# Frequency filter and SwiGLU block on one Trainium2 core: the inverse transform's last stage on 32x32 parts, in one burst a chunk

## Chip, cores and metric

One Trainium2 chip, one core. The metric is device time in microseconds of one launch, the median of three runs. The engines carry their usual names: TensorE (PE in the profile, its weight loads PEld), VectorE (DVE), ScalarE (ACT), GpSimd (POOL) and SyncE (SP), which issues most of the DMAs. Each engine works through its own instructions in order and waits on semaphores for the others.

## What is computed

The reference does two things, one after the other, all in float32:

```python
X = np.fft.rfft(x, axis=1)                       # x: (8, 3008, 256)
y = np.fft.irfft(X * (filt_r + 1j * filt_i)[None], n=3008, axis=1)
x = y.reshape(24064, 256)
g, val = x @ w_gate, x @ w_val                   # 256 -> 1536
out = (g * sigmoid(g) * val) @ w_out             # 1536 -> 256
```

The weights arrive as float64 and are rounded on the chip at the start. There are 8 batches of 3008 tokens.

## The kernel before

**Two pipelines in one order.** For each batch the filter is a Fourier transform written as matrix products. 3008 is 47 x 64, so there is a first stage over 47 points, a second over 64, the filter, and the same two backwards. While the block after it (the SwiGLU products) works on batch b, the transforms of batch b + 1 are slipped in between. A batch's tokens are cut into 4 chunks (`NCHUNK`), the hidden units into 3 groups (`NG`), so a batch takes 12 steps, and step s works on chunk s // 3 and group s % 3.

**The order is written by hand.** Every step goes once through the list `SCHEDULE`, token by token, and each token issues a few instructions on their engines; `pin` keeps them in that order. A quote at the end of a token (`S00'`) means the step before. These are the tokens that matter here:

- `P`, `Q`, `A`, `B`, `E` are products with the weights on TensorE (four records of 188 columns each). The pairs 01, 02, ... belong to a scheme that saves products at the price of sums.
- `f`, `c`, `m`, `g`, `u` are ScalarE's copies and SiLUs. `x`, `s`, `y`, `e`, `l` prepare or correct a PSUM bank on VectorE or ScalarE. So `s13` (or `x03`) must be done before product `A13` can add to its bank.
- `h` and `v` are VectorE's products of the two halves of a pair. They fill the two `h` tiles of the step. `h03` and `v03` are the last of a step.
- `S00` to `S31` are GpSimd's sums of `h` slots, `D` its differences, and `W1` to `W7` are the products with `w_out`, which read `h` and those sums a step later. `o` and `z` gather their results, `x0.o` to `x5.o` and `i` store them.
- `n1`, `n2`, `n3` call `combine_sequence`: sums of a new chunk's `y` into `y_t`, which A, B and E products read.
- `t0.0` to `t4.3` and `b0` to `b7` take one piece each of the next batch's transforms, from the lists `plan` and `bursts`. `quads` (first stage, steps 0 to 3) and `fours` (second stage and its inverse, steps 4 to 10) come through `b`; `first_fold` in step 11.

At the end of a step the order is `E03 n1 t4.1 v01 g23 B03 l03 W3 h23 g03 u03 h03 v03`, and the next one begins `Q0 o3' z1.o' t4.2' W2 b0 f0 S00' S01' i0 b1 b2`.

**The stage that changes.** `back(k, m)` is the inverse's last step, 47 points from 24 frequencies, for chunk k. Its input is tile `t4` (`load_t4`, two tiles a chunk, read from DRAM with two DMAs each: one for the tokens with h = 0 on partitions 0 to 47, one for h = 1 on partitions 64 to 111). On each half the 24 cosine rows and 24 sine rows lie one below the other, so one product of 48 rows yields 32 of the 47 points: m = 0 gives points 0 to 31, m = 1 points 15 to 46 (`LATER` = 15; the overlap is computed twice). Table `back_t` holds the two 48 x 32 tables for each half. One call issues 16 products (2 tiles x 4 channel parts x 2 halves; each fp32 product shows as two matmul records) into 2 PSUM banks. Two VectorE transposes of 32 x 32 blocks (L1049) bring these into `y`. After m = 1 GpSimd makes four sums in place in `y` (the lines at L312 and L315 for `y<-y`), which the products need.

The calls are placed by `plan`: for chunks 1, 2, 3 in steps 1, 4 and 7 of their batch, m = 0 at `t2.0` and m = 1 at `t3.1`; for chunk 0 in step 11 of the batch before, at `t0.0` and `t2.0`. `t4` is loaded at the head of steps 0, 2, 5 and at `B01` in the same steps; chunk 0's in step 10 at `A12` and `E23`. Batch 0 uses another routine (`stage3`) and isn't touched, but its step 11 holds batch 1's first chunk.

Of the kernel before, what the change touches and what calls it, by code (L numbers as in the profile page):

```python
# [41 lines left out]
FP32 = mybir.dt.float32  # L42
# [11 lines left out]
N1, N2 = 47, 64  # L54
# [31 lines left out]


SCHEDULE = """
Q0 o3' z1.o' t4.2' W2 b0 f0 S00' S01' i0 b1 b2 x0.o' t0.0 x1.o' i1 Q1 P0 t0.1 x2.o' P3 x3.o' f1 t4.3'
W1 x4.o' S10' x03 S11' D01 i2 i3 i4 s13 b3 x5.o' P1 o1 b4 t0.2 o2 z0.o c1 i5 A13 g1 c0 S20' Q2  # L90
S21' g0 y01 m13 t1.0 h0 f2 s01 W6 t1.1 h1 x23 D02 P2 o6 D12 A01 t0.3 i6 c2 i7 B13 i8 g2 i9 n3' m01
i10 S30' t1.2 i11 x02 W7 S31' g13 y12 y02 B01 h13 o7 t1.3 t2.0 s02 s12 g01 h2 b5 Q3 t2.1 h01 e12
A02 y23 W4 e02 b6 y03 m02 g3 A12 o4 z2.o t2.2 E12 m12 B02 t2.3 l12 e13 b7 E02 u12 g02 t3.0 h3 s23
l02 B12 v12 E13 t3.1 h02 u02 A23 n2 l13 g12 v02 W5 s03 e23 h12 e01 m23 A03 o5 z3.o u13 E23 t3.2 m03
v13 E01 l23 e03 t3.3 t4.0 l01 u23 B23 v23 u01 E03 n1 t4.1 v01 g23 B03 l03 W3 h23 g03 u03 h03 v03
""".split()
KS = (-1, 0, 1, 2)

# [11 lines left out]
SLOT = {p: i for i, p in enumerate(ORDER)}  # L110
SUM = {f"{z}{i}{j}": 6 * e + n for e, z in enumerate("ABE") for n, (i, j) in enumerate(PAIRS)}
NPR = len(ORDER)

LATER = N1 - 32

PIECES = ((0, 7), (7, 14), (14, 20), (20, 26))

# [4 lines left out]
def dft_tables():  # L122
# [27 lines left out]
    hi = 2 * np.pi * (np.outer(2 * n1 + 1, s) % (2 * N1)) / (2 * N1)  # L150
    scale = np.where(s == 0, 1.0, 2.0) / S
    one_hi = np.concatenate([np.cos(hi) * scale, -np.sin(hi) * scale * (s > 0)], 1).T
    back = np.zeros((128, 2, 32))
    for h, table in enumerate((one, one_hi)):
        for m in range(2):
            back[64 * h:64 * h + 2 * NS, m] = table[:, LATER * m:LATER * m + 32]
    back = back.reshape(128, 64)

    quad = np.zeros((4, 32, 2, 32))
    for h in range(2):  # L160
# [40 lines left out]
def kernel(  # L201
# [357 lines left out]
    def load_back():  # L559

        t = rpool.tile([128, 2, 128], U32, name="quad", tag="pw", bufs=3)
        t = t.bitcast(FP32).rearrange("p b f -> p (b f)")
        quad_t.append(t)
        pin(nc.sync.dma_start(out=t[:, 0:65], in_=quad_dram.ap()))
        t = rpool.tile([128, 2, 128, 2], U32, name="back", tag="raw", bufs=2)
        t = t.bitcast(FP32).rearrange("p b f two -> p (b f two)")
        back_t.append(t[:, 0:64])
        pin(nc.sync.dma_start(out=back_t[0], in_=back_dram.ap()))


# [10 lines left out]
    class Spectral:  # L581
# [82 lines left out]
        def load_t4(self, k, i, part=None):  # L664
            at = 2 * k + i
            if part:
                self.load_rows(self.t4[k, i][8 * N_STORED:NK], k, slice(2 * N_STORED, NS), ts(i, NH))
                return
            t = t4pool.tile([128, NH, C], FP32, name=f"t4_{self.b}_{k}_{i}", tag="t4")
            if part == 0:  # L670
                self.load_rows(t[0:8 * N_STORED], k, slice(0, 2 * N_STORED), ts(i, NH), nc.gpsimd)
            elif self.b == 0:
                self.load_rows(t[0:NK], k, slice(0, NS), ts(i, NH))
            else:

                rows = self.d2_tokens.rearrange("(h n) a c -> h a n c", h=2)
                for h in range(2):
                    self.load(out=t[64 * h:64 * h + 2 * NS], in_=rows[h, :, ts(at, NH)])
            self.t4[k, i] = t

        def bank(self, name):
# [346 lines left out]

        def back(self, k, m):

            if m == 0:
                self.y[k] = ypool.tile([128, 8, TQ], FP32, name=f"y_{self.b}_{k}", tag="y")
            y = self.y[k]
            banks = [bank(f"pd_{self.b}_{k}_{m}_{h}") for h in range(2)]
            outs_ = [t.rearrange("p (z i n d) -> p i z n d", z=2, i=2, d=32) for t in banks]
            for i in range(2):
                t = self.t4[k, i].rearrange("p n (z j d) -> p j z n d", z=2, d=32)
                for j in range(4):  # L1040
                    for h in range(2):
                        r = slice(64 * h, 64 * h + 2 * NS)
                        pin(nc.tensor.matmul(  # L1043
                            out=outs_[h][32 * j:32 * j + 32, i], lhsT=back_t[0][r, ts(m, 32)],
                            rhs=t[r, j], start=i == 0, stop=True, skip_group_check=True))
            yield
            to = y.rearrange("p s n -> p (s n)").rearrange("p (z h m r) -> p h z m r", z=2, h=2, r=N1)
            for h in range(2):
                pin(nc.vector.transpose(  # L1049
                    out=to[:, h, :, :, LATER * m:LATER * m + 32],  # L1050
                    in_=banks[h].rearrange("p (z m d) -> p z m d", z=2, d=32)))
                if h == 0:
                    yield
            for a in range(4 if m else 0):
                b, v = y[:, a], y[:, 4 + a]
                for _ in range(abs(KS[a])):
                    pin((sub if KS[a] > 0 else add)(nc.gpsimd, v, v, b))
# [33 lines left out]
    class Group:  # L1091
# [94 lines left out]
        def project(self, op, last=False):  # L1186
# [9 lines left out]
            if kind in "xXi":  # L1196
                t, cb, step = outs[b, k], int(kind == "X"), 2 if last else 1
                if kind == "x" and q < NG - 1 and takes_turns(b, k) and p == 5:
                    pin(nc.sync.dma_start(out=o_dram[k], in_=t))
                if q == NG - 1 and (b or kind == "i"):  # L1200
                    some = (p,) if kind == "i" else (2 * p, 2 * p + 1)
                    for n, (u, cq) in enumerate(divmod(m, 4) for m in some):
                        rows = min(32, NR - 32 * u)
                        at = (b * S + 32 * 32 * u + 2 * NH * k) * C + 128 * cb + 32 * cq
                        queue = nc.sync if b else nc.gpsimd
                        if last:
                            queue = (nc.sync, nc.scalar, nc.gpsimd)[(2 * p + n) % 3]
                        pin(queue.dma_start(  # L1208
                            out=bass.AP(tensor=out.tensor, offset=out.offset + at,
                                        ap=[[32 * C, rows], [128 * step, 4 * NH // step], [1, 32]]),  # L1210
                            in_=t[32 * cq:32 * cq + rows, cb::step, ts(u, 32)]))
                return
# [159 lines left out]


    older = before = None
    gap = iter(())
    pieces_before = []

    def order_of(b):
# [24 lines left out]
            yield  # L1403


    def later(piece):

        yield
        yield from piece

    def chain(*pieces):

# [30 lines left out]
    for b in range(B):  # L1443
# [2 lines left out]
        plan = [[] for _ in range(NCHUNK * NG)]  # L1446

        def three(s, k, cur=cur):
            if s.b == 0:
                return [s.stage3(k, step) for step in range(4)]  # L1450
            return [s.back(k, m) for m in range(2)]

        d = [three(cur, k) for k in range(1, NCHUNK)]
        one = [] if b else [nxt.stage1(u) for u in range(N_ONE)]
        bursts = [[] for _ in range(NCHUNK * NG)]
        if b and nxt:
            for n in range(N_QUAD // 2):
                bursts[n] = nxt.quads(n)
            for n in range(N_FOUR + 1):
                bursts[N_QUAD // 2 + n] = nxt.fours(n)  # L1460
        if b + 2 < B:
            bursts[-1] = following.first_fold()
        bursts = [iter(p) for p in bursts]
        two = []
# [2 lines left out]
            two += [nxt.stage2a(u)] if u < N_TWO else []  # L1467
        if nxt:
            gap = iter(())
            first = three(nxt, 0)  # L1470
            plan[11] = [first[0], gap, first[1]]
            if b:
                plan[1], plan[4], plan[7] = [[gap, gap, p[0], later(p[1])] for p in d]
            if b == 0:
                for k in range(NCHUNK - 1):
                    plan[k] = d[k] + one[k:k + 1]
                plan[0] = [gap, d[0][0], chain(d[0][1], d[0][2]), d[0][3], one[0]]
                plan[3], plan[4], plan[5] = one[3:8], one[8:13], one[13:16]
# [3 lines left out]
        else:  # L1482
            plan[1], plan[4], plan[7] = [[gap, gap, p[0], later(p[1])] for p in d]

        for step in range(NCHUNK * NG + (b == B - 1)):
            ghost = step == NCHUNK * NG
# [15 lines left out]
            for place, token in enumerate(SCHEDULE):  # L1502
                if b == 0 and this and place in tick_at[min(step, 3)]:
                    preparation.tick(step)
                old = token.endswith("'")
# [14 lines left out]
                elif op[0] == "t":  # L1520
                    n = int(op[1])
                    ps = pieces_before if old else pieces
                    if n < len(ps):
                        next(ps[n], None)
                elif op[0] == "b":
                    next(bursts[step] if this else gap, None)
                elif op[0] in "Wo" or op.endswith(".o"):
# [19 lines left out]
                if b and chunk and op == "B01":  # L1547
                    cur.load_t4(chunk, 1)
                for i in range(2):
                    if nxt and (step, op) == (10, ("A12", "E23")[i] if b else "E23"):  # L1550
                        nxt.load_t4(0, i)
                for f, args in chores.get((step, op), ()) if b == 0 else ():
                    f(*args)
                if op in ends and not last and (b or step >= NT * NG - 1):
                    reload_weights((g + 1) % NG, ends[op])
            older, before, pieces_before = before, this, pieces
    for op in LAST:
# [32 lines left out]
```

## Time and profile before

| | |
|---|---|
| median of three runs | 2787.48 us (2787.07 to 2790.02) |
| profiled execution | 2790.41 us |
| its span, first to last instruction | 2788.6 us |
| mean granted TensorE clock | 0.997 |
| records of `back` (L1043) | 1792 matmuls, mean 382 ns, busy 61.4 us |
| transposes of `back` (L1049) | 112, mean 707 ns |
| sums in `y` on GpSimd | 112 of 188 elements, 0.59 to 0.61 us each |
| loads of `t4` (`t<-d`) | 112 of 192 KB on SP's queue |

The profile is of one execution. Its first part gives busy time by engine. "Busy" counts a matmul from its start to its modelled end, and matmuls overlap, so TensorE's 99% is no measure of how fast it goes; the distance from one start to the next is. The chain is the work that ended last, followed back from the end: at each step to whatever released it. Groups (line, engine, operation, output<-inputs, shape, count) give busy time, mean duration of one, and the idle time before them. A timeline lists instructions by start, with equal neighbours merged; the brackets behind a row tell how long the engine had been idle and what ended that.

W2 stands near the head of every step (`wF<-h` in the profile), so the distance between two of its starts is the length of a step.

### The profile page before, as it was taken

How to read it: one execution, taken by the hardware profiler on the slowest of the kernel's cores; microseconds unless marked ns; L12 is line 12 of the kernel's file. 1: busy time of each engine (PE TensorE's matmuls, PEld its weight loads, DVE VectorE, ACT ScalarE, POOL GpSimd, SP SyncE). 2: the span in 40 equal slices, each digit the busy share in tenths (PEclk: the TensorE clock that was granted, in tenths of full speed). 3: DMA queues.
4: the chain of work that ended last, by engine and by line, in shares of the span. 5: the costliest groups of instructions: out<-in, count | busy, mean ns of one | idle time of the engine just before them, and what ended most of it. 6: DMA issues, size and time to landing. Idle time of an engine off the chain costs nothing.

```text
span 2788.6 us, 51410 instructions
## 1 busy us (share of the span) xinstructions
PE 2748.3 (99%) x16952; PEld 2249.3 (81%) x16952; DVE 2081.7 (75%) x4703; ACT 1514.6 (54%) x4086; POOL 1647.4 (59%) x1801
## 2 busy tenths in 40 slices
PE   8999999999999999999999999999999999999998
PEld 6777887888878888788878888878887888888886
DVE  7888777777687777777778777777777777676666
ACT  5776454555555555555555555555554555555553
POOL 4786576566545665556654566555655566555554
PEclk9999999999999999999999999999999999999999
DMA  8688877878676776777767777668767677655543
GB/s 216 218 273 267 282 240 243 265 243 263 205 211 208 253 244 190 212 238 229 247 184 233 220 249 223 207 194 264 243 213 201 215 239 237 183 156 147 156 137 83
DMA packets 383488, 608.47 MB, mean 218 GB/s; under 512 B 197118, under 2 KB 266652, under 8 KB 383048
## 3 DMA queue, kind: packets, MB, share of 16 engines
q1 hardware_dynamic: 364410, 574.18, 65.9%
q10 hardware_dynamic: 16174, 25.50, 3.6%
q0 software_dynamic: 2640, 5.51, 0.7%
q8 instruction: 137, 2.24, 0.3%
q14 instruction: 127, 1.04, 0.1%
HBM read 484.45 MB, written 118.12 MB: 216 GB/s over the span
## 4 chain that ended last, share of the span: by engine, by line
PE 89%; DVE 3%; POOL 2%; ACT 1%; DMA 1%; issue 1%; SPq 0%; POOLq 0%; DVEq 0%; ACTq 0%
PE wa L1125 25%; PE wk L1125 17%; PE wA L1223 16%; PE we L1125 12%; PE wG L1223 8%; PE wF L1223 4%; PE wpd L1043 2%; PE wqc L807 1%; PE wqb L819 1%; PE wqa L727 1%; POOL h L315 0%; POOL out_dram L1208 0%; PE wpa L889 0%; DVE we L315 0%; DVE y L319 0%
## 5 line engine op out<-in xcount | busy, mean ns | idle before, releaser
L1125 PE MATMUL wa<-y_t,wt_t 128*128 128x188 f32 x4464 | 883.5, 324 | 10.5 <-DVE wa L1147 5.5
L1125 PEld LDWEIGHTS wa<-y_t,wt_t 128*128 128x128 f32 x4464 | 746.0, 190 | 102.9 <-issue 14.7
L1125 PEld LDWEIGHTS wk<-y,wt_t 128*128 128x128 f32 x2976 | 494.4, 190 | 125.2 <-issue 36.7
L1125 PE MATMUL wk<-y,wt_t 128*128 128x188 f32 x2976 | 575.6, 326 | 1.4 <-ACT f L1140 1.4
L315 POOL TENSOR_TENSOR h<-h 128x376 f32<-128x376 f32 x572 | 560.1, 1000 | 15.1 <-DVE h L312 14.9
L1223 PE MATMUL wA<-h,wo_t 128*128 128x376 f32 x1532 | 549.0, 481 | 3.4 <-POOL h L315 1.8
L1125 PE MATMUL we<-y_t,wt_t 128*128 128x188 f32 x2232 | 432.4, 323 | 2.4 <-DVE we L319 1.6
L315 POOL TENSOR_TENSOR D<-f,f 128x376 f32<-128x376 f32 x288 | 280.5, 985 | 252.0 <-ACT f L1140 245.4
L312 POOL TENSOR_TENSOR h<-h 128x376 f32<-128x376 f32 x190 | 183.2, 984 | 408.0 <-DVE h L1172 402.2
L315 DVE TENSOR_TENSOR we<-we,m 128x376 f32<-128x376 f32 x576 | 317.3, 552 | 91.6 <-PE we L1125 51.4
L1125 PEld LDWEIGHTS we<-y_t,wt_t 128*128 128x128 f32 x2232 | 369.1, 190 | 4.9 <-DVE we L319 2.8
L1223 PEld LDWEIGHTS wA<-h,wo_t 128*128 128x128 f32 x1532 | 278.0, 190 | 106.6 <-POOL h L315 5.4
L1160 ACT COPY m<-wa 128x376 f32<-128x376 f32 x576 | 275.4, 478 | 110.8 <-PE wa L1125 105.0
L1167 ACT ACTIVATE u<-we 128x188 f32<-128x188 f32 x576 | 188.9, 328 | 188.5 <-DVE we L315 179.1
L1223 PE MATMUL wG<-h,wo_t 128*128 128x376 f32 x768 | 273.9, 479 | 0.0
L319 DVE SCALAR_TENSOR_TENSOR y<-wk,c 128x376 f32<-128x376 f32 x480 | 246.7, 540 | 33.7 <-ACT c L1144 29.5
L1167 ACT ACTIVATE g<-wa 128x188 f32<-128x188 f32 x576 | 187.4, 326 | 143.8 <-PE wa L1125 141.6
L1144 ACT COPY c<-wk 128x376 f32<-128x376 f32 x288 | 136.9, 475 | 234.5 <-PE wk L1125 228.1
L1156 ACT COPY we<-y 128x376 f32<-128x376 f32 x480 | 218.9, 480 | 42.9 <-DVE y L1049 24.7
L1140 ACT ACTIVATE f<-wk 128x376 f32<-128x376 f32 x288 | 145.1, 504 | 168.6 <-PE wk L1125 108.3
L1172 DVE TENSOR_TENSOR h<-we,u 128x188 f32<-128x188 f32 x576 | 198.7, 345 | 35.1 <-ACT u L1167 21.9
L1172 DVE TENSOR_TENSOR h<-wa,g 128x188 f32<-128x188 f32 x576 | 196.1, 344 | 26.2 <-ACT g L1167 26.1
(194 smaller groups left out, 3532.0 us busy)
## 6 DMA issues: line engine op xcount, KB each, us to landing
wt_t<-w_all SPq DMA_DIRECT2D x174, 896.0 KB
wt_t<-w_all SPq DMA_DIRECT2D x174, 768.0 KB
lent<-filter SPq DMA_DIRECT2D x36, 1024.0 KB
quads<-lent SPq DMA_DIRECT2D x96, 256.0 KB
d<-lent ACTq DMA_DIRECT2D x84, 256.0 KB
t<-d SPq DMA_DIRECT2D x112, 192.0 KB
lent<-quads SPq DMA_DIRECT2D x144, 128.0 KB
lent<-raw SPq DMA_DIRECT2D x144, 128.0 KB
```

The costliest lines, as they stand in the source:

```text
L312: return eng.tensor_tensor(out=dst, in0=a, in1=b, op=ALU.add)
L315: return eng.tensor_tensor(out=dst, in0=a, in1=b, op=ALU.subtract)
L319: return nc.vector.scalar_tensor_tensor(out=dst, in0=a, scalar=-1.0, in1=b, op0=ALU.mult, op1=ALU.subtract)
L1043: pin(nc.tensor.matmul(out=outs_[h][32 * j:32 * j + 32, i], lhsT=back_t[0][r, ts(m, 32)], rhs=t[r, j], start=i == 0, stop=True, skip_group ...
L1125: pin(nc.tensor.matmul(out=ps[:, z], lhsT=self.wt[:, SLOT[p], z], rhs=rhs, start=start and z == 0, stop=True, skip_group_check=True))
L1140: pin(act.mul(self.small(f"f{i}", f"f{i}", 1), t[f"k{i}"], -1.0))
L1144: pin(act.copy(out=self.small(f"c{i}", f"c{i}", 1), in_=t[f"k{i}"]))
L1156: pin(act.copy(out=self.bank(f"e{at}"), in_=t[f"y{at}"]))
L1160: pin(act.copy(out=self.small(f"m{at}", "m", 4), in_=t[f"a{at}"]))
L1167: pin(act.activation(out=self.small(op, "g", 3, 1)[:, 0], in_=ps[:, 1], func=AF.Silu))
L1172: pin(v.tensor_tensor(out=dst, in0=ps[:, 0], in1=g, op=ALU.mult))
L1223: pin(nc.tensor.matmul(out=self.tiles[at], lhsT=wo_t[:, JB * q + i, WO[p], :], rhs=self.hs[i][:, HID[p]], start=start and i == 0, stop=Tru ...
```

## The change

1. `back` takes a whole chunk in one call. Cosine and sine rows are parted: `t4` is loaded with four DMAs a tile, 24 rows each, to partitions 0, 32, 64 and 96 (h = 0 cosine, h = 0 sine, h = 1 cosine, h = 1 sine), and `back_t` holds four 24 x 24 tables. Each of four parts gives 24 points, and 32 products (2 x 4 x 4, 32 columns of output, 24 rows in, 256 columns long) go to four PSUM banks.
2. The cosine banks are transposed by VectorE straight into `y`. The sine banks are copied to SBUF by ScalarE and transposed there in place by VectorE. Then GpSimd makes points 24 to 46 as cosine minus sine, mirrored, and points 0 to 23 as cosine plus sine in place, four sums a chunk. The four old sums in `y` follow.
3. New tokens `r0` to `r5` place the pieces. `r0` (the burst) stands between `l03` and `W3` at the end of steps 0, 3, 6 (chunks 1, 2, 3) and 10 (chunk 0 of the next batch); `r1` (transposes and copies) before `h03`; `r2'` to `r5'` in the step that follows. The calls in `plan` go. Batch 1's chunk 0 goes through `bursts` in step 11 of batch 0, beside `first_fold`.
4. Chunk 0's `t4` is loaded in step 10 at `B01` and `A12`.
5. In the very last stores, the second half of the channels (`X`) goes to the queues of SP and ACT only, no longer to GpSimd's.

```diff
-Q0 o3' z1.o' t4.2' W2 b0 f0 S00' S01' i0 b1 b2 x0.o' t0.0 x1.o' i1 Q1 P0 t0.1 x2.o' P3 x3.o' f1 t4.3'
+Q0 o3' z1.o' t4.2' W2 b0 f0 S00' S01' i0 b1 b2 x0.o' r2' t0.0 x1.o' i1 Q1 P0 t0.1 x2.o' P3 x3.o' f1 t4.3'
...
-i10 S30' t1.2 i11 x02 W7 S31' g13 y12 y02 B01 h13 o7 t1.3 t2.0 s02 s12 g01 h2 b5 Q3 t2.1 h01 e12
-A02 y23 W4 e02 b6 y03 m02 g3 A12 o4 z2.o t2.2 E12 m12 B02 t2.3 l12 e13 b7 E02 u12 g02 t3.0 h3 s23
+i10 S30' t1.2 i11 x02 W7 S31' g13 y12 r3' y02 B01 r4' h13 o7 t1.3 t2.0 s02 s12 g01 h2 b5 Q3 t2.1 h01 e12
+A02 y23 W4 e02 b6 y03 m02 g3 A12 o4 z2.o t2.2 E12 m12 B02 t2.3 l12 e13 b7 E02 r5' u12 g02 t3.0 h3 s23
...
-v13 E01 l23 e03 t3.3 t4.0 l01 u23 B23 v23 u01 E03 n1 t4.1 v01 g23 B03 l03 W3 h23 g03 u03 h03 v03
+v13 E01 l23 e03 t3.3 t4.0 l01 u23 B23 v23 u01 E03 n1 t4.1 v01 g23 B03 l03 r0 W3 h23 g03 u03 r1 h03 v03
...
-    back = np.zeros((128, 2, 32))
+    back = np.zeros((4, 32, 32))
     for h, table in enumerate((one, one_hi)):
-        for m in range(2):
-            back[64 * h:64 * h + 2 * NS, m] = table[:, LATER * m:LATER * m + 32]
-    back = back.reshape(128, 64)
+        back[2 * h:2 * h + 2, 0:NS, 0:NS] = table.reshape(2, NS, N1)[:, :, 0:NS]
+    back = back.reshape(128, 32)
...
-                rows = self.d2_tokens.rearrange("(h n) a c -> h a n c", h=2)
-                for h in range(2):
-                    self.load(out=t[64 * h:64 * h + 2 * NS], in_=rows[h, :, ts(at, NH)])
+                rows = self.d2_tokens.rearrange("(h n) (r s) c -> h r s n c", h=2, r=2)
+                for part in range(4):
+                    self.load(out=t[32 * part:32 * part + NS],
+                              in_=rows[part // 2, part % 2, :, ts(at, NH)])
...
+        def back(self, k):
+
+            self.y[k] = y = ypool.tile([128, 8, TQ], FP32, name=f"y_{self.b}_{k}", tag="y")
+            banks = [bank(f"pd_{self.b}_{k}_{part}") for part in range(4)]
+            views = [t.rearrange("p (z i n d) -> p i z n d", z=2, i=2, d=32) for t in banks]
             for i in range(2):
                 t = self.t4[k, i].rearrange("p n (z j d) -> p j z n d", z=2, d=32)
                 for j in range(4):
-                    for h in range(2):
-                        r = slice(64 * h, 64 * h + 2 * NS)
+                    for part in range(4):
+                        r = slice(32 * part, 32 * part + NS)
                         pin(nc.tensor.matmul(
-                            out=outs_[h][32 * j:32 * j + 32, i], lhsT=back_t[0][r, ts(m, 32)],
+                            out=views[part][32 * j:32 * j + 32, i], lhsT=back_t[0][r],
                             rhs=t[r, j], start=i == 0, stop=True, skip_group_check=True))
             yield
             to = y.rearrange("p s n -> p (s n)").rearrange("p (z h m r) -> p h z m r", z=2, h=2, r=N1)
+            odd = []
             for h in range(2):
                 pin(nc.vector.transpose(
-                    out=to[:, h, :, :, LATER * m:LATER * m + 32],
-                    in_=banks[h].rearrange("p (z m d) -> p z m d", z=2, d=32)))
-                if h == 0:
-                    yield
-            for a in range(4 if m else 0):
+                    out=to[:, h, :, :, 0:32],
+                    in_=banks[2 * h].rearrange("p (z m r) -> p z m r", z=2, r=32)))
+                t = xpool.tile([128, NV, C], FP32, name=f"odd_{self.b}_{k}_{h}", tag="x")
+                odd.append(t.rearrange("p i c -> p (i c)"))
+                pin(nc.scalar.copy(out=odd[h], in_=banks[2 * h + 1]))
+            yield
+            for t in odd:
+                pin(nc.vector.transpose(out=t, in_=t))
+            yield
+            for h in range(2):
+                t = odd[h].rearrange("p (z m r) -> p z m r", z=2, r=32)
+                n, low = slice(1 - h, 1 - h + N1 - NS), to[:, h, :, :, 0:NS]
+                pin(sub(nc.gpsimd, to[:, h, :, :, N1 - 1:NS - 1:-1],
+                        to[:, h, :, :, n], t[:, :, :, n]))
+                pin(add(nc.gpsimd, low, low, t[:, :, :, 0:NS]))
+                yield
+            for a in range(4):
...
-                            queue = (nc.sync, nc.scalar, nc.gpsimd)[(2 * p + n) % 3]
+                            queue = (nc.sync, nc.scalar, nc.gpsimd)[(2 * p + n) % (3 - cb)]
...
+        backs = {3 * k - 3: cur.back(k) for k in range(1, NCHUNK)} if b else {}
+        if b and nxt:
+            backs[10] = nxt.back(0)
...
+        if b == 0:
+            bursts[-1] = side_by_side(nxt.back(0), following.first_fold())
...
-            first = three(nxt, 0)
-            plan[11] = [first[0], gap, first[1]]
-            if b:
-                plan[1], plan[4], plan[7] = [[gap, gap, p[0], later(p[1])] for p in d]
...
+                elif op[0] == "r":
+                    next(back_before if old else backs.get(step, gap), None)
...
-                    if nxt and (step, op) == (10, ("A12", "E23")[i] if b else "E23"):
+                    if nxt and (step, op) == (10, ("B01", "A12")[i] if b else "E23"):
```

More of the change, by code (lines that the diff above doesn't have):

```diff
@@ L112 @@
 NPR = len(ORDER)
-LATER = N1 - 32
 PIECES = ((0, 7), (7, 14), (14, 20), (20, 26))
@@ L566, in load_back @@
         t = t.bitcast(FP32).rearrange("p b f two -> p (b f two)")
-        back_t.append(t[:, 0:64])
+        back_t.append(t[:, 0:32])
         pin(nc.sync.dma_start(out=back_t[0], in_=back_dram.ap()))
@@ L1027, in stage3 @@
                         out=v, in0=b, scalar=-float(k), in1=c, op0=ALU.mult, op1=ALU.add))
[L1031 to L1037, printed above, removed]
+        def back(self, k):
+            self.y[k] = y = ypool.tile([128, 8, TQ], FP32, name=f"y_{self.b}_{k}", tag="y")
+            banks = [bank(f"pd_{self.b}_{k}_{part}") for part in range(4)]
+            views = [t.rearrange("p (z i n d) -> p i z n d", z=2, i=2, d=32) for t in banks]
             for i in range(2):
@@ L1374 @@
     older = before = None
-    gap = iter(())
+    gap = back_before = iter(())
     pieces_before = []
@@ L1403, in sooner, with side_by_side @@
             yield
-    def later(piece):
-        yield
-        yield from piece
+    def side_by_side(*pieces):
+        for _ in range(8):
+            for piece in pieces:
+                next(piece, None)
+            yield
     def chain(*pieces):
@@ L1448, in three @@
         def three(s, k, cur=cur):
[L1449 to L1453, printed above, removed]
+            return [s.stage3(k, step) for step in range(4)]
+        d = [three(cur, k) for k in range(1, NCHUNK)] if b == 0 else []
+        backs = {3 * k - 3: cur.back(k) for k in range(1, NCHUNK)} if b else {}
+        if b and nxt:
+            backs[10] = nxt.back(0)
         one = [] if b else [nxt.stage1(u) for u in range(N_ONE)]
@@ L1460 @@
                 bursts[N_QUAD // 2 + n] = nxt.fours(n)
-        if b + 2 < B:
+        if b == 0:
+            bursts[-1] = side_by_side(nxt.back(0), following.first_fold())
+        elif b + 2 < B:
             bursts[-1] = following.first_fold()
@@ L1481 @@
                 plan[6][0] = sooner(plan[6][0])
-        else:
-            plan[1], plan[4], plan[7] = [[gap, gap, p[0], later(p[1])] for p in d]
         for step in range(NCHUNK * NG + (b == B - 1)):
@@ L1501 @@
             last = ghost or b == B - 1 and step == NCHUNK * NG - 1
-            for place, token in enumerate(SCHEDULE):
+            place = -1
+            for token in SCHEDULE:
+                place += token[0] != "r"
                 if b == 0 and this and place in tick_at[min(step, 3)]:
@@ L1556 @@
             older, before, pieces_before = before, this, pieces
+            back_before = backs.get(step, gap)
     for op in LAST:
```

## The prediction

> **What bounds the kernel now.** I read the page's first part and its chain, then the timeline of TensorE over three steps of the last batch, then the timelines of single step ends. The page says who sets the time:
>
> ```profile
> PE 2748.3 (99%) x16952; PEld 2249.3 (81%) x16952; DVE 2081.7 (75%) x4703; ACT 1514.6 (54%) x4086; POOL 1647.4 (59%) x1801
> PE 89%; DVE 3%; POOL 2%; ACT 1%; DMA 1%; issue 1%; SPq 0%; POOLq 0%; DVEq 0%; ACTq 0%
> ```
>
> TensorE carries 89% of the chain; no other engine carries over 3%. How tightly it is packed shows in the timeline of TensorE, batch 7 (start, duration in us, line; `wF` is W2 at the head of a step, `wpd` a burst of `back`):
>
> ```profile
> 2483.53 1.43 PE L1223 MATMUL wF<-h,wo_t 128*128 128x376 f32 x4
> ...
> 2495.05 1.09 PE L1043 MATMUL wpd<-t,back 48*32 48x256 f32 x32
> ...
> 2502.62 1.09 PE L1043 MATMUL wpd<-t,back 48*32 48x256 f32 x32
> ...
> 2511.37 1.43 PE L1223 MATMUL wF<-h,wo_t 128*128 128x376 f32 x4
> ...
> 2536.77 1.43 PE L1223 MATMUL wF<-h,wo_t 128*128 128x376 f32 x4
> ```
>
> A step with `back` takes 2511.37 - 2483.53 = 27.84, the next one, without, 25.40. The two bursts cost 2.44, 1.22 each: 1.02 in the chain and some 0.2 because the product behind them starts late. Nothing hides them, so a microsecond off TensorE is a microsecond off the kernel, and one added wait likewise.
>
> **TensorE's part of the change.** The pair (two bursts of 16 fp32 products, 32 matmul records each, 8 tiles of 48x32) becomes one burst of 32 products, 64 records, on 16 tiles of 32x32. Per tile, 64/16 = 4 records of 256 columns follow each other, as 32/8 = 4 did in one old burst. So one new burst should last about as long as one old one, if 16 tiles do run beside each other and issuing keeps up. The nearest row is the existing 16-tile stage (`wqa`, 24x32, 2 records of 512 columns deep); chain, then weight loads:
>
> ```profile
> 915.00 1.02 PE wpd L1043 x32
> ...
> 925.10 1.02 PE wqc L807 x16
> ...
> 1119.88 1.07 PE wqa L727 x32
> ```
> ```profile
> 1119.81 0.23 PEld L727 LDWEIGHTS wqa<-lent,quad 24*32 24x32 f32 x32 [0.53 <-issue]
> ```
>
> 16 records of 4 tiles (`wqc`), 32 of 8, 32 of 16, all 1024 columns deep, take 1.02 to 1.07: depth counts, not the number of records. 32 loads of 0.103 each lie in 0.23, so they start some 4 ns apart. The cost of a new burst: 1.07 + 0.20 = 1.27. Bounds: 1.22 (an old burst) and 2.44 (a tile count that doesn't help). I take 1.27, the row with the same tile count. Gain 2.44 - 1.27 = 1.17 a chunk; `back` runs for 4 chunks of 7 batches, 28 times: 28 x 1.17 = 32.8.
>
> [...]
>
> **The other engines, by sum.** VectorE: 4 transposes from PSUM (L1049, 0.707 each) become 2 of those and 2 in place in SBUF (nearest row: `o<-o` 128x384, 0.56; 512 columns some 0.69): 2.8 either way. ScalarE: 2 copies 128x512 a chunk, 0.59 each by `lent<-wqa` L738: +1.2. GpSimd: 4 sums of 368 or 384 elements, 0.98 to 1.00 by its 128x376 rows: +4.0 a chunk, 112 in all. For strided, reversed views no row exists; 2 us each is my upper bound, 0.6 (the 188-element rows) the lower. GpSimd's timeline has it idle from 824 to 836 in the step that begins at 811.4, and it does them there. In step 11 it is tight: today the sums into `y_t` run until the next S00 begins (1117.76). S31 ends 12.6 after W2 (1090.14), 11.3 without the burst that leaves; from there 4.0 + 2.3 (the four old sums in place) + 3.1 + 4.2 (`y_t`) end at 24.9, where the shorter step wants S00 at 25.4 - 0.9 = 24.5. That is 0.4 late, and W6, the first to need those sums, leaves 4. At 2 us a sum it would be 4.4 late and just touch W6. SP: `load_t4` issues 4 DMAs instead of 2, 112 more of some 0.45, same bytes. They stand far ahead (in step 10 now at B01 and A12, some 15 before the burst); behind them on SP wait weight pieces that aren't needed for 10 or more. Nothing.
>
> **Waits at the end of a step.** The burst needs 4 banks; the last is freed by v01, whose row ends at 809.09, before W3's start at 809.49, which is where the burst begins. Its 2 transposes stand ahead of h03 and v03 on VectorE. From W3's old start: burst to 1.10, transposes to 2.49, h03 to 2.74, v03 to 3.02. W2's second half, which needs v03, comes at 1.27 + 1.26 (W3) + 0.64 (Q0) + 0.63 = 3.80. Spare 0.8; if the transposes took twice as long, W2 would wait 0.6 at each of the 28 ends, 17 in all. S00' starts at 2.8 and the fourth sum ends at 6.6, before D01 (f1 at 7.3). Nothing.
>
> **Waits at the head of the next step.** Here the two in-place transposes (r2') are ahead of x03 and s13 on VectorE, and A13 on TensorE waits for s13. VectorE, end of a step 0, then TensorE:
>
> ```profile
> 814.65 0.69 DVE L315 TENSOR_TENSOR lent<-lent,wqa 128x512 f32<-128x512 f32 x1 [2.07 <-ACT lent L738]
> 815.37 0.69 DVE L312 TENSOR_TENSOR lent<-lent,wqa 128x512 f32<-128x512 f32 x1
> 816.04 0.55 DVE L1147 SCALAR_TENSOR_TENSOR x<-wk,f 128x376 f32<-128x376 f32 x1
> 816.50 0.55 DVE L1147 SCALAR_TENSOR_TENSOR wa<-wk,f 128x376 f32<-128x376 f32 x1
> ```
> ```profile
> 817.74 0.80 PE L1125 MATMUL wa<-y_t,wt_t 128*128 128x188 f32 x4
> ```
>
> s13 ends at 817.05, A13 starts at 817.74: 0.69 to spare. With the transposes (start to start 0.50 at 384 columns, so 0.63): two sums at 5.16 + 1.27 = 6.43 and 7.15, transposes 7.82 and 8.45, x03 9.08, s13 9.54 to 10.09; A13 wants 8.25 + 1.27 = 9.52. Wait 0.6. VectorE then has no gap until s01 (820.14 to 820.68; A01 at 820.91), so another 0.47. A step 0's end costs 1.07. The same sum after step 6 (sums at 981.76 and 982.48, L837 at 983.09, A13 at 985.80) gives a wait of 0.2; after step 3 (only L837 at 897.83, A13 at 900.91) none, 0.13 to spare; after step 10 and in batch 7 the transposes run before x03 can. In batches 1 to 6: 6 x (1.07 + 0.2) = 7.7. Bounds: 0 if VectorE's order loosens, 6 x 3 = 18 if the same lag hits all three.
>
> Step 11 gives something back: it takes 27.84 to 29.27 today where 27.84 is due, partly because an old transpose (1097.42) stands before s01. That transpose leaves. I count 0.4 in 5 batches, 2.0 (0 to 5). The tail's last stores leave GpSimd's queue (0.6 an issue) for two others (0.45 each): +0.4, bounds -0.5 and 1.
>
> Sum: 32.8 - 7.7 + 2.0 + 0.4 = 27.5. The profiled execution took 2790.4, span 2788.6; 2790.4 - 27.5 = 2762.9. It lies 2.9 above the median 2787.48, which becomes 2760.0.
>
> **Rivals.** (A) Sixteen tiles help half as much: a burst costs 1.9, gain 28 x 0.54 - 5 = 10; 2777. The equal 1.02 rows speak against it. (B) Slower, by VectorE's queue at the head of a step: each in-place transpose waits out a GpSimd sum of 1.0, so s13 comes 2.0 later. Then step 0's end costs 3.1, step 6's 2.2, step 3's 1.9: 6 x 7.2 = 43 against 35.2 of gains; 2795. It decides once the extra lag passes 1.6 a step end. For: GpSimd runs S10 to S21 just then. Against: `o<-o`, in place too, stands at 811.54 in 1.04 for two, under S01 and S10 on GpSimd, unhindered. [...] (C) No waits at all: 2787.5 - 35.2 = 2752.
>
> **How the numbers follow.** Forecast (waits as summed, 2752 to 2769) 0.75, with C in its lower end; A, or all three step ends waiting, 2769 to 2782: 0.12; between, no change 0.05; B 0.08. The likeliest gives 2760. The range 2751 to 2775 takes in no waits and waits of 18 with a slightly dearer burst. Measurement tells 0.2%, 5.6 us: faster 0.87, same 0.05, slower 0.08.
>
> **What would show it.** Right: `wpd` once a chunk, 64 records in 1.0 to 1.2; steps 4 and 7 of batch 7 at 25.4 and the step that ends in a burst 26.7; steps 1 to 2 of batches 1 to 6 at 26.7 plus 1.1. The waits before `wa` at the head of steps 1 and 7 go to VectorE. Wrong: a burst of 2 us, a TensorE wait on v03 before W2, `o<-o` or `odd` transposes of over 1 us, GpSimd late with S00 in step 11.

## The result and the profile after

| | before | after |
|---|---|---|
| median, side by side on one chip (7 runs each) | 2788.35 us | 2773.00 us (2768.80 to 2779.17) |
| ratio after / before | | 0.9947, 95% interval 0.9932 to 0.9961 |
| profiled execution | 2790.41 us | 2773.0 us |
| its span | 2788.6 us | 2771.2 us |

The change makes the kernel faster by 0.53%, 15.4 us by the medians and 17.4 by the profiled executions. The forecast was 27.5. So the sign was right and the time, 2773.0, lies at the upper end of the range, above the span of 2752 to 2769 that the likeliest case had: over a third of the gain did not come.

The page after says that the bound is unchanged: TensorE still carries the chain, and the sums of the other engines moved as summed (GpSimd 110.6 more, 28 x 4.0 = 112 forecast; VectorE level), but for ScalarE (20.6 more, 28 x 1.2 = 33.6 forecast).

```profile
PE 2728.7 (98%) x16952; PEld 2243.7 (81%) x16952; DVE 2082.3 (75%) x4703; ACT 1535.2 (55%) x4142; POOL 1758.0 (63%) x1909
PE 87%; DVE 4%; ACT 2%; DMA 2%; POOL 1%; issue 1%; SPq 0%; ACTq 0%; POOLq 0%; DVEq 0%
```

The timeline of TensorE in the last batch, cut to W2 (`wF`) and the burst (`wpd`); start and duration in us. This batch has no other transform work beside it, so its steps show the burst alone:

```profile
2469.66 1.43 PE L1232 MATMUL wF<-h,wo_t 128*128 128x376 f32 x4
2495.05 1.43 PE L1232 MATMUL wF<-h,wo_t 128*128 128x376 f32 x4
...
2520.76 1.43 PE L1232 MATMUL wF<-h,wo_t 128*128 128x376 f32 x4
2544.35 1.49 PE L1039 MATMUL wpd<-t,back 24*32 24x256 f32 x64
2547.78 1.43 PE L1232 MATMUL wF<-h,wo_t 128*128 128x376 f32 x4
```

The plain step is 2495.05 - 2469.66 = 25.39, as before. The one with the burst is 2547.78 - 2520.76 = 27.02. The burst costs 1.62, where the old pair cost 2.44 and the forecast had 1.27. The weight loads of the same burst say where to look. Before, the existing 16-tile stage issued 32 loads in 0.23 us. Now 64 take 1.01:

```profile
2544.34 1.01 PEld L1039 LDWEIGHTS wpd<-t,back 24*32 24x32 f32 x64 [0.22 <-issue]
```

Twice the records take four times as long. The single records show how: records 1 to 16 start 6.7 ns apart (0 to 0.100 us), 17 to 32 likewise (0.240 to 0.340), number 33 at 0.456, number 34 only at 0.649, and from there nearly all follow at 16.7 ns, up to 1.120. 27 of the 28 bursts have this pattern; in the first, in step 11 of batch 0, a wait for a load of `t4` comes on top.

At the head of a step the forecast waits are there. VectorE in step 1 of batch 2, whose W2 starts at 808.30, then TensorE:

```profile
812.89 1.30 DVE L1054 STREAM_TRANSPOSE odd<-odd 128x512 f32<-128x512 f32 x2
814.11 0.51 DVE L1156 SCALAR_TENSOR_TENSOR x<-wk,f 128x376 f32<-128x376 f32 x1
814.54 0.55 DVE L1156 SCALAR_TENSOR_TENSOR wa<-wk,f 128x376 f32<-128x376 f32 x1
```
```profile
814.01 0.80 PE L1134 MATMUL wk<-y,wt_t 128*128 128x188 f32 x4
815.24 0.88 PE L1134 MATMUL wa<-y_t,wt_t 128*128 128x188 f32 x4 [0.42 <-DVE wa L1156]
```

The two in-place transposes run at 0.67 to 0.70 each, beside GpSimd's sums, and s13 (the `wa<-wk,f` row) ends at 815.09. A13 starts at 815.24, 1.23 after the `wk` product before it; two such starts are 0.64 apart when nothing waits. So A13 loses 0.6. A01, which starts 0.14 after s01 ends (818.78 after 818.64), loses the rest of the 1.04 that the next table shows for this step.

Step lengths (W2 to W2, batches 2 to 4) of the kernels below; 512 is the version with products of 512 columns, "last" the version with all three repairs:

| step | before | after | 512 | last | what differs |
|---|---|---|---|---|---|
| 1 | 29.11 | 27.70 | 27.70 | 26.66 | pair gone; in-place transposes ahead of s13 |
| 3 | 26.75 | 28.37 | 28.02 | 28.02 | a burst at its end |
| 4 | 29.06 | 26.62 | 26.62 | 26.62 | pair gone, no wait |
| 6 | 27.48 | 29.10 | 28.75 | 28.75 | a burst at its end |
| 7 | 29.92 | 27.79 | 27.79 | 27.48 | as step 1 |
| 10 | 26.62 | 28.24 | 27.89 | 27.89 | a burst at its end |
| 11, batches 1 to 5 | 28.3 to 29.3 | 25.5 to 27.4 | 25.5 to 27.4 | 25.5 | two bursts gone; a wait that comes and goes |

### The profile page after: what moved, and what is told of

Its sections match the earlier page's. It is cut to its first block, busy times and chain, and to the rows that moved or that the text cites. A ratio compares the mean times of both kernels' runs of the same rounds, so it can differ in the third digit from the quotient of the medians.

```text
span 2771.2 us, 51629 instructions
## 1 busy us (share of the span) xinstructions
PE 2728.7 (98%) x16952; PEld 2243.7 (81%) x16952; DVE 2082.3 (75%) x4703; ACT 1535.2 (55%) x4142; POOL 1758.0 (63%) x1909
## 4 chain that ended last, share of the span: by engine, by line
PE 87%; DVE 4%; ACT 2%; DMA 2%; POOL 1%; issue 1%; SPq 0%; ACTq 0%; POOLq 0%; DVEq 0%
PE wa L1134 24%; PE wk L1134 16%; PE wA L1232 16%; PE we L1134 12%; PE wG L1232 8%; PE wF L1232 4%; PE wpd L1039 1%; PE wqc L805 1%; PE wqb L817 1%; PE wqa L725 1%; DVE we L312 1%; DVE y L316 0%; DVE lent L312 0%; DMA y<-y 0%; DVE h L1181 0%
## 5 line engine op out<-in xcount | busy, mean ns | idle before, releaser
L1134 PEld LDWEIGHTS wk<-y,wt_t 128*128 128x128 f32 x2976 | 497.3, 190 | 111.2 <-issue 27.5
L1181 DVE TENSOR_TENSOR h<-we,u 128x188 f32<-128x188 f32 x576 | 199.0, 346 | 38.0 <-ACT u L1176 24.9
```

The lines of the kernel that those rows point to most:

```text
L1134: pin(nc.tensor.matmul(out=ps[:, z], lhsT=self.wt[:, SLOT[p], z], rhs=rhs, start=start and z == 0, stop=True, skip_group_check=True))
L1181: pin(v.tensor_tensor(out=dst, in0=ps[:, 0], in1=g, op=ALU.mult))
```

## The experiments

Each kernel was run beside the kernel before; times are medians, ratios go against that kernel on the same chip. Two theories stood for the burst: that the waits on the DMAs of `t4`'s second tile, which fall into its middle, break its issue, or that TensorE has only so many records ready and is fed slowly beyond.

**1. No wait in mid burst.** `t4` becomes one constant tile of two halves (`t4_all`), and the products are split by z instead of by i, so that the first four already wait for everything.

```diff
-    t4pool = pool("t4", 2)
+    t4_all = cpool.tile([128, 2, NH, C], FP32)
...
-            t = t4pool.tile([128, NH, C], FP32, name=f"t4_{self.b}_{k}_{i}", tag="t4")
+            t = t4_all[:, i]
...
+            t = t4_all.rearrange("p i n (z j d) -> p z j (i n) d", z=2, d=32)
+            for z in range(2):
...
+                            rhs=t[r, z, j], start=z == 0, stop=True, skip_group_check=True))
```

> The changed kernel with both halves of t4 in one constant tile, and the burst's 32 products split by the z half of the columns instead of by the t4 tile: as before 64 records of 256 columns on 16 tiles, but the first products read both halves, so every DMA wait stands ahead of the burst and none in its middle. Theory W (the waits on the second t4 tile, in the middle of the burst, break its issue): the burst costs 1.27 of the step instead of 1.62, 28 x 0.35 = 9.8 us, so about 2763 where the changed kernel has 2773. Theory Q (TensorE is fed at some 17 ns a record beyond the first 32, whatever the waits): the burst stays at 1.5 to 1.62 and the time at 2769 to 2774.

Measured: 2773.52 us, ratio 0.9947 (0.9935 to 0.9960), the same as the changed kernel. The burst is the same to some nanoseconds, record 34 at 0.650 included:

```profile
2548.28 1.50 PE L1039 MATMUL wpd<-t_all,back 24*32 24x256 f32 x64
```

The waits in mid burst have no part in it. Theory W falls.

**2. Half the records, the same columns.** `t4_all` is as in 1; one product takes both halves.

```diff
+            t = t4_all.rearrange("p i n (z j d) -> p j z (i n) d", z=2, d=32)
+            for j in range(4):
...
+                        out=banks[part][32 * j:32 * j + 32], lhsT=back_t[0][r],
+                        rhs=t[r, j], start=True, stop=True))
```

> The changed kernel with both halves of t4 in one constant tile and one product for both: 16 products of 512 columns, 32 records on 16 tiles, the same columns in all and no wait in mid burst. Theory W and theory Q both expect a burst that costs 1.27 (the last batch's step with a burst 26.67 instead of 27.02), 9.8 us less, about 2763. A third theory, that 16 tiles with this table and these moving data are slower in themselves, expects 1.6 and no gain. If the next loads of t4, which now reach a tile whose two halves are both still in use, came late, TensorE would show waits on the DMAs of t4 at the ends of steps 3, 6 and 10.

Measured: 2766.08 us, ratio 0.9914 (0.9901 to 0.9928), 0.0033 or 9 us less than the changed kernel; expected were 9.8. The timeline of TensorE in the last batch:

```profile
2516.72 1.43 PE L1231 MATMUL wF<-h,wo_t 128*128 128x376 f32 x4
2540.31 1.14 PE L1038 MATMUL wpd<-t_all,back 24*32 24x512 f32 x32
2543.39 1.43 PE L1231 MATMUL wF<-h,wo_t 128*128 128x376 f32 x4
```

The step takes 26.67, the burst 1.27, which is the forecast's figure: with the record count of the row that it was taken from, the row holds. The 32 records start at 0 to 0.100 and 0.454 to 0.554, and W3 behind them at 1.071 instead of 1.424.

**3. The other way: 128 records.** Each product of the changed kernel is cut in two by z, 128 columns each.

```diff
+                for z in range(2):
...
+                                out=views[part][32 * j:32 * j + 32, i, z], lhsT=back_t[0][r],
+                                rhs=t[r, j, z], start=i + z == 0, stop=True, skip_group_check=True))
```

> The changed kernel with each of the burst's products cut in two: 64 products of 128 columns, 128 records, the same columns and the same 16 tiles. Theory Q (only some 32 records stand ready, the others are fed at some 17 ns each): the last of 128 records starts at about 0.4 + 96 x 0.0167 = 2.0 us, the burst costs 2.4 to 2.6 of the step instead of 1.62, 28 x 0.9 = 25 us more, about 2798. A theory in which the columns per tile set the burst's length expects 1.3 to 1.6 and 2764 to 2773.

Measured: 2795.68 us, ratio 1.0011 (1.0002 to 1.0020), by the ratios 18 us more than the changed kernel: all of the change's gain is gone. The burst costs 27.43 - 25.40 = 2.03 in the last batch, not 2.4 to 2.6: behind the first 32 (up to 0.234) the other 96 come at 14.6 ns on average, up to 1.634. That is 28 x 0.41 = 11.5. The rest I had not expected. The profile puts 6.4 us of idle time inside bursts, in four places, to `issue`: TensorE stood still and waited for no engine and no data that is shown. 11.5 and 6.4 make the 18. Waits of TensorE (total, times, longest), then its timeline around the longest:

```profile
PE wpd L1040 <- issue: 6.4, 4, 2.9
```
```profile
2147.91 1.77 PE L1040 MATMUL wpd<-t,back 24*32 24x128 f32 x113
2152.54 0.68 PE L1040 MATMUL wpd<-t,back 24*32 24x128 f32 x15 [2.87 <-issue]
```

The DMA packets of the same trace tell what ended these four: TensorE went on 1.30, 1.34, 1.36 and 1.43 us after a packet of 16 KB on queue q8, which the page lists under `instruction`, had landed. There are 130, 137 and 151 such packets with 32, 64 and 128 records a burst; the last step is 14 x 16 KB for 3584 more weight loads and matmuls, 64 bytes each. So TensorE was most likely waiting for its own instructions to be read.

The columns in all and the tiles are the same in the three versions, and the cost rises 1.27, 1.62, 2.03 with the records. Theory Q holds in kind; its rate was sized too slow.

**4. The in-place transposes behind s13**, on the changed kernel.

```diff
-Q0 o3' ... b2 x0.o' r2' t0.0 x1.o' ...
+Q0 o3' ... b2 x0.o' t0.0 x1.o' ...
-W1 x4.o' S10' x03 S11' D01 i2 i3 i4 s13 b3 ...
+W1 x4.o' S10' x03 S11' D01 i2 i3 i4 s13 r2' b3 ...
```

> The changed kernel with the two in-place transposes put on VectorE's queue behind x03 and s13 of the next step instead of ahead of them. The prediction's reading of the waits: step 1 of batches 1 to 6 takes 26.7 instead of 27.70 and step 7 27.48 instead of 27.79, 6 x (1.03 + 0.31) = 8.0 us less, about 2765. Rival: VectorE has no slack anywhere in these steps, and the 1.2 us of transposes delay the next sum that TensorE waits for (s01, y01) as much: no gain, 2773. A second rival: GpSimd gets the transposed halves 1.5 us later, its four sums run into S20 and S21, and D01 or D02 come late: waits on GpSimd, a loss.

Measured: 2777.77 us, ratio 0.9957 (0.9944 to 0.9971): no gain; the interval overlaps that of the changed kernel. Step 7 drops to 27.48 as expected, but step 1 takes 27.77. VectorE, then TensorE in step 1 (W2 at 815.99):

```profile
821.56 1.29 DVE L1054 STREAM_TRANSPOSE odd<-odd 128x512 f32<-128x512 f32 x2
...
825.84 0.55 DVE L1156 SCALAR_TENSOR_TENSOR wa<-wk,D 128x376 f32<-128x376 f32 x1
```
```profile
822.34 0.80 PE L1134 MATMUL wa<-y_t,wt_t 128*128 128x188 f32 x4
...
826.54 1.51 PE L1134 MATMUL wa<-y_t,wt_t 128*128 128x188 f32 x8 [0.86 <-DVE wa L1156]
```

A13 no longer waits (6.35 after W2 instead of 6.94), but A01 does, which needs s01 (the `wa<-wk,D` row): it starts 10.55 after W2 instead of 10.48. The first rival was right for step 1: the 1.3 us are too much anywhere ahead of s01. Step 11 loses too (26.7 to 27.4 in batches 1 to 5, 3.4 in all more than in the changed kernel): in batches 1 to 4 VectorE's first sum for the next transform, at `b4`, waits for no DMA, but now stands behind the moved transposes and ahead of s01.

**5. Both of these**: the diffs of 2 and 4 together.

> The one product of 512 columns for both halves of t4, and the in-place transposes behind x03 and s13, together. If the burst's extra 0.35 and the waits at the head of steps 1 and 7 are all that separates the changed kernel from its forecast without waits, 9.8 + 8.0 = 17.8 less: about 2755. If the shorter burst gives VectorE less time, so that waits come back elsewhere, 2758 to 2763.

Measured: 2770.33 us, ratio 0.9924 (0.9910 to 0.9937), no better than 512 columns alone. Step 1 takes 27.77, the step with a burst 26.66 in the last batch: the two edits add up step by step, and the second is worth nothing.

**6. The transposes behind s01**, with 512 columns; `r2'` leaves its place as in 4.

```diff
-S21' g0 y01 m13 t1.0 h0 f2 s01 W6 ...
+S21' g0 y01 m13 t1.0 h0 f2 s01 r2' W6 ...
```

> The one product of 512 columns for both halves of t4, and the two in-place transposes behind s01 of the next step on VectorE, two sums later than in the version that put them behind s13. Behind s13 the wait at the head of step 1 only moved to A01, which waits for s01 (27.77 instead of 27.70 a step 1, 27.48 instead of 27.79 a step 7). If the 1.3 us of transposes are what is too much ahead of s01, step 1 of batches 1 to 6 now takes 26.6 to 26.8 and step 7 27.48: 6 x (1.0 + 0.3) = 8 us under the 2766.1 of the 512-column version alone, about 2758. GpSimd reaches the first sum with the turned halves 13.2 us after W2 and the transposes would end some 12.5 after it, so the sums wait for nothing. Rival: VectorE is short of time in the whole step and the wait moves on to B01 or y01: no gain, 2766.

Measured: 2770.41 us, ratio 0.9926 (0.9914 to 0.9939): a miss for the sum and a hit for the steps. Step 1 takes 26.66 and step 7 27.48, as expected. But step 11, where VectorE has little to do at the head, takes 27.6 to 27.8 in batches 1 to 5, 4.7 in all more than in the profile of 512 columns alone, and batch 0, whose length differs by several us between runs of all these kernels, took 4.5 more.

**7. Placed by step**: behind s01, but at the head in step 11. `r2'` stays where the change has it, and `r6'` stands behind s01.

```diff
+                elif op in ("r2", "r6") and (step == 11) != (op == "r2"):
+                    pass
                 elif op[0] == "r":
```

> The 512-column product, with the in-place transposes behind s01 in all steps but step 11, where they stay at the head of the step. Putting them behind s01 everywhere took 1.04 off step 1 and 0.31 off step 7 as expected, but step 11, where VectorE has nothing else to do at the head, became 27.6 where the 512-column version has 25.5 to 27.4. Kept apart by step, both hold: step 1 26.66, step 7 27.48, step 11 25.5 to 27.4 as before; 6 x 1.35 = 8.1 under the 512-column version's ratio of 0.9914 (2766), about 2758, ratio 0.9885. If batch 0, whose DMA waits differ by 4 us from run to run, decides more than that, the profile's steps still show it.

Measured: 2761.02 us, ratio 0.9890 (0.9874 to 0.9907); expected 0.9885. Steps 1 and 7 hold and step 11 is 26.9 in four batches and 29.7 in one.

**8. The fold sums one place later.** What the slow step 11 waits for shows in batch 1 of the version of experiment 7; VectorE, then TensorE:

```profile
757.27 0.69 DVE L309 TENSOR_TENSOR lent<-lent 128x512 f32<-128x512 f32 x1 [3.05 <-DMA lent<-in_x_dram]
...
759.06 0.55 DVE L1155 SCALAR_TENSOR_TENSOR wa<-wk,D 128x376 f32<-128x376 f32 x1
```
```profile
759.75 2.54 PE L1133 MATMUL wa<-y_t,wt_t 128*128 128x188 f32 x7 [2.31 <-DVE wa L1155]
```

The first sum of the next transform's input (`lent<-lent`, a fold sum, issued by `first_fold`) stands in VectorE's queue ahead of s01, and its rows of x, loaded at the head of the same step, land late. This version starts the fold at `b5` instead of `b4` and adds a token `b8` (two lines that count the pieces and tokens go with it).

```diff
         def first_fold(self):
-            for _ in range(4):
+            for _ in range(5):
...
-... E23 t3.2 m03
+... E23 t3.2 m03 b8
```

> The version with the transposes placed by step, and in step 11 the four fold sums on VectorE (two inputs in SBUF) each one place later, so that none stands ahead of s01. In the profiles step 11 takes either 25.5 or 26.7 to 27.4; in the slow ones the first fold sum, beside a GpSimd sum, takes 0.9 to 1.57 instead of 0.68, s01 behind it is late and TensorE waits 0.6 to 0.8 for A01, and about as much 12 us later. If that fold sum is the cause, step 11 is 25.5 in batches 1 to 5 and this version is 3 to 7 us faster than the other, about 2753. If the order of GpSimd's sums is the cause, step 11 stays at 26.7 or more in most batches and the time at 2758.

Measured, on the same chip as 7: 2754.44 us, ratio 0.9870 (0.9855 to 0.9885), 6.6 us less. Step 11 takes 25.53 in all of batches 1 to 5. My expectation had the cause half right: the sum's place ahead of s01 is what matters. But by the row above what it waits for is first a DMA. The overlap with GpSimd is real and comes on top: in the 512-column version such a sum waited 0.35 for the DMA and then took 1.57 instead of 0.68.

**9. More GpSimd work** on the changed kernel, to test the cover that the prediction claimed.

```diff
-                pin(sub(nc.gpsimd, to[:, h, :, :, N1 - 1:NS - 1:-1],
-                        to[:, h, :, :, n], t[:, :, :, n]))
+                for _ in range(3):
+                    pin(sub(nc.gpsimd, to[:, h, :, :, N1 - 1:NS - 1:-1],
+                            to[:, h, :, :, n], t[:, :, :, n]))
```

> The changed kernel with the first of each half's two GpSimd sums done three times over (it writes the same values each time): 4 more sums of some 0.95 a chunk on GpSimd, 28 x 3.8 = 106 us of work, as much again as the change itself added there. The prediction's reading: GpSimd is idle enough in the steps that begin behind a burst, and in step 11 the sums into y_t end 4 us later, just where W6 would need them: 0 to 3 us more in all, 2773 to 2776. Rival: VectorE's fold sums with two inputs in SBUF give way to GpSimd's sums, each overlap costs up to 1 us, and TensorE waits for it: 10 us or more.

Measured: 2789.17 us, ratio 0.9990 (0.9978 to 1.0001), 12 us more than the changed kernel. Steps 1 to 10 are unchanged to 0.3 us: there the cover holds. The loss sits at step 11 (27.4 in all of batches 1 to 5, 34.6 instead of 30.2 in batch 0) and in the step 0 behind it (29.9 instead of 29.2). The prediction's reading misses by far, and the rival has the size. In step 0 it has the cause as well: the fold sum ahead of s01 takes 1.35 to 1.39 beside a GpSimd sum in batches 1 to 5, where it takes 0.68 in the changed kernel, and A01, which needs s01, waits (0.78 in batch 2). In step 11 not all of the loss need be the added sums': the first fold sum waited for its DMA in all five batches (0.20 to 1.16), as it does in some batches of the other runs.

**10. ScalarE's part undone**, on the changed kernel.

```diff
-                pin(nc.scalar.copy(out=odd[h], in_=banks[2 * h + 1]))
-            yield
-            for t in odd:
-                pin(nc.vector.transpose(out=t, in_=t))
+                pin(nc.vector.transpose(out=odd[h], in_=banks[2 * h + 1]))
+            yield
             yield
```

> The changed kernel with ScalarE's part undone: VectorE transposes the two sine halves straight from their PSUM banks, as it does the cosine halves, four transposes at the step's end and none in place. By the prediction's sum W2's second half, which needs v03, has 0.75 to spare now (v03 ends at 808.18, that product is due at 808.93), and two more transposes of 0.70 ahead of h03 and v03 make W2 wait 0.6 at each of 28 step ends, 17 more; the waits at the heads of steps 1 and 7 leave, 8.0 less: about 2782. Rival: if h03 and v03 are not as close as that, only the 8.0 show: 2765.

Measured: 2784.40 us, ratio 0.9970 (0.9959 to 0.9981); expected 2782. W2's second half now waits for v03 at 27 of 28 step ends; waits of TensorE, then its timeline in the last batch:

```profile
PE wF L1230 <- DVE h L1179: 8.7, 27, 0.3
```
```profile
2554.94 0.80 PE L1230 MATMUL wF<-h,wo_t 128*128 128x376 f32 x2
2556.06 0.90 PE L1230 MATMUL wF<-h,wo_t 128*128 128x376 f32 x2 [0.32 <-DVE h L1179]
```

The second half starts 1.12 behind the first, where 0.63 is due. By step lengths the wait is 0.59 (27.21 instead of 26.62 in step 4), 16.5 in 28 steps, beside a prediction of 0.6. So the copies by ScalarE are worth their instructions: they buy this step end for a smaller wait in the next step.

## Why the prediction was half right, step by step

- **The burst, 1.27: wrong, and the main miss.** The step that failed is "about as long as one old one, if 16 tiles do run beside each other and issuing keeps up". The tiles did run beside each other (32 records of 512 columns on the same 16 tiles cost 1.27 in experiment 2), but the issue did not keep up: record 33 starts at 0.456 and record 64 at 1.120. The line "depth counts, not the number of records" was read from rows of 16 and 32 records and carried to 64. It measured 1.62: a gain of 0.82 a chunk instead of 1.17, 23.0 in 28 instead of 32.8. The 9.8 that are missing make up most of the 12 between forecast and median. Experiments 1 to 3 show that the count does it; that only some 32 records stand ready in front of TensorE is my reading of the pattern, and no trace shows it directly. In this trace each record is a weight load and a matmul, the first 32 start within 0.340, and number 34 is the first late one, 0.19 behind number 33.
- **Waits at the head of the next step, 7.7: right.** Without them step 1 takes 26.66 and step 7 27.48 (experiment 7), so they were 1.04 and 0.31, predicted 1.07 and 0.2. Batch 1's step 1 lost only 0.32 (27.95 against 27.63). The sum is 5 x 1.04 + 0.32 + 6 x 0.31 = 7.4. (Even so, 27.63 is 0.96 above the 26.67 that batch 1's step 1 took before without its pair; no experiment tells why.) Step 4 takes 26.62 in the versions with ScalarE's copies, but for one step of experiment 3: no wait, as said.
- **Step 11, a gain of 2.0: 0.3 came.** The sum counts the old transpose ahead of s01 and leaves out that the fold sum, also ahead of s01, waits for its DMA. In batches 1 to 5 the excess over the plain step is 4.3 before (28.62, 28.31, 28.85, 28.46 and 29.27 less 27.84 each) and 4.0 after (27.44, three times 25.53 and 27.01 less 25.40). Before, the fold sum waited for x in all five (0.05 to 1.20 us); after, in two (1.77 and 1.32), and these two steps hold 3.65 of the 4.0. Where it hardly waited, the excess is 0.47 before (batch 2) and 0.13 after (batches 2 to 4). So something like the 0.4 a batch that was counted for the transpose is there, though no run takes the transpose out alone; how late the load comes outweighs it. The wait was on record in the profile of before:

```profile
L312 DVE TENSOR_TENSOR lent<-lent 128x512 f32<-128x512 f32 x48 | 36.1, 753 | 4.6 <-DMA lent<-in_x_dram 4.5
```

- **The tail, 0.4, and GpSimd, VectorE and SP at nothing.** From the last W2 to the end of the span it is 17.8 before and 18.0 after: nothing gained. The new GpSimd sums, on strided and reversed views, take what the row of 376 elements said:

```profile
L309 POOL TENSOR_TENSOR y<-y,odd 128x384 f32<-128x384 f32 x56 | 56.7, 1012 | 4.4
L312 POOL TENSOR_TENSOR y<-y,odd 128x368 f32<-128x368 f32 x56 | 56.1, 1002 | 0.0
```

  In step 11 they make GpSimd late: S00 starts at 1111.91, 25.92 after W2. The sum had 24.9, where 24.5 was due; so it is 1.4 late instead of 0.4. The step behind lost nothing by it. But the slack of 4 that I read from W6 was not the limit: about 4 us more of sums cost 0.7 in step 0, at A01 and not at W6, through a VectorE sum that took 1.35 to 1.39 instead of 0.68 beside a GpSimd sum (experiment 9). The prediction's sum has no term for this overlap.
- **The rivals.** Rival A's burst of 1.9 was nearer in time than in kind: the tiles help in full, the feed does not. Rival B, in-place transposes that wait out GpSimd's sums, is refuted: 56 of them take 0.67 to 0.70. Rival C had no waits, and they were there.
- **The whole.** 23.0 - 7.4 + 0.3 makes 15.9 of the 17.4 between the profiled executions, but the parts don't fall where that says. From step 0 of batch 1 to the end, the profiles differ by 13.1: 22.1 from 27 bursts and 0.3 in step 11, less 7.4 of waits, 0.2 in the tail and some 1.8 of small losses that no term has (1.0 in step 1 of batch 1, 0.5 in the steps 2, 0.4 in the steps 5 and 8). The other 4.3 lies ahead of that. 0.8 of it is the 28th burst. The remaining 3.5 is luck, as far as these profiles tell: it lies in batch 0, which the change leaves alone up to its step 11, and W2 of that step starts at 418.9 before, 414.2 after, and anywhere from 412 to 423 in the other versions.

The version with all three repairs (512 columns, transposes by step, fold later) beats both kernels: 0.9870 against 0.9947 is 21.5 us. From the profiles: bursts 28 x 0.36 = 10.1, waits at steps 1 and 7 of 7.4, step 11 of 4.0 - 0.65 = 3.4, together 20.9.

## What to carry to other kernels

When many small products are packed onto tiles, count instructions as well as columns: up to 32 records ran here at the price of the rows with 16, and beyond that they followed each other at 14.6 to 16.7 ns with 256 columns or with 128, so prefer fewer, longer products (two buffers side by side in one tile made 512 columns out of twice 256). A row's price holds for its count too; when the new work has twice the records of the row it is priced by, take that as an unknown with an upper bound of its own.

On an engine that works in order, what matters is which wait stands ahead of the instruction that the bound engine needs next. Moving 1.3 us of work behind s13 gained nothing in step 1, moving it behind s01 gained 1 us a time there, and in step 11 both moves lost.

## What the hardware showed that was not expected

- A burst of 64 records on 16 tiles has a gap of 0.19 us behind record 33 and then a pace of 16.7 ns, against 6.7 ns before; with 128 records the 96 late ones averaged 14.6 ns.
- With 128 records a burst, TensorE stopped in four places for up to 2.9 us, with no wait on another engine or on data shown. Each time it went on 1.30 to 1.43 us after 16 KB on the `instruction` queue q8 had landed.
- Beside GpSimd sums, VectorE's sums with two inputs in SBUF took up to 1.57 us in the version with 512 columns and up to 1.29 in the profile after, instead of 0.68, while its in-place transposes, with one input, stayed at 0.67 to 0.70 in the profile after. The same sums with one input in PSUM (`lent<-lent,wqa`) took 0.67 to 0.69 there, 75 of the 96 beside GpSimd.
